# A feature product and a low part on GpSimd, two projections in other empty PSUM banks, query rows loaded first, and instruction lists found anew

## The chip, the cores and the metric

The program runs on one core of one Trainium2 chip. Its time is the device time of one execution in microseconds; the time before is the median of three runs, 313.84 us (313.17 to 314.41).

## The reference

Linear attention is followed by a gated spatial layer, for 4 batches (b), 4 heads, 1088 rows (s) and a head width of 32, all in float32:

```python
a = einsum('rd,bhsd->bhsr', S1, x)                  # 8 features
b = einsum('rd,bhsd->bhsr', S2, x)                  # 8 features
phi(x) = a[..., :, None] * b[..., None, :]          # 64 feature products
q_p, k_p = phi(q), phi(k)
kv = einsum('bhsf,bhsd->bhfd', k_p, v);  z = sum of k_p over s
x  = (q_p . kv) / (q_p . z + 1e-6)                  # joined over heads: (b, s, 128)
h  = relu(x @ w_in);  u, v = h[..., :512], h[..., 512:]
v_n = layer norm of v over its 512 columns
v_s = einsum('ts,bsd->btd', w_spatial, v_n) + b_spatial
out = (u * v_s) @ w_out
```

## The kernel before

**Order.** Every operation is written once with `op(engine, cost, function, reads, writes)` (class `Order`). The text `SEQ` lists all 1922 operations as `name:number@engine`. From it each of five engines (PE, ACT, DVE, POOL and SP, which issues nearly all DMAs) takes its own list and works through it strictly in order, so an operation that waits holds up all that stands behind it in its list. The engine in `SEQ` may be any of an operation's `alts`. `RANK` says in which order the tiles of one tag take the buffers of that tag. A planner's costs decide only where idle PE is given filler matmuls (`FILL`, line 638).

**Stages.** Batch 0 opens the kernel (`attention0`): key rows `kt00` to `kt02` (three groups of 384 rows), values `v00` to `v02` and query rows `qt00` to `qt02` are loaded; `phi` projects a group with the 64 columns of `sk` into a PSUM bank (`kab00`, `qab00`, line 781, 6 matmuls of full float32, which the trace shows as 12 records); ACT copies the a half to SBUF (`ka00`, line 786); DVE multiplies it with the b half, which it reads from PSUM (`kp00`, `qp00`, line 788, 768 products a partition). PE sums keys and values (`kv0:1` to `kv0:3`, line 818), DVE masks the sum (`kd0`, line 842), PE turns the query features (`tq00`, line 863), ACT copies them (`qpT00`, line 867), PE multiplies (`nd00`, line 877), DVE divides (lines 881 to 884), PE turns the result (`xt0`, line 891), and ACT and DVE split it into a high part `xh` and a low part `xl`. Before all that PE runs warm-up matmuls on zeros (`wps`, lines 629 and 633).

**Then** the layer: `pv` (lines 606 to 608, three matmuls for a product of high and low parts), its norm on DVE and ACT, `pu`, the large spatial sums `sp` (lines 1172 to 1183) and the output `po`. The first batch's weights come in meanwhile: `wi_raw1` and `wi_raw0` are halves of `w_in` in float64, turned to float32 in seven steps (`wi_x1:1` to `:7`, lines 673 to 687) and split into `wih` and `wil` (lines 693 and 614 to 617); `wt` are pieces of the spatial matrix, split into `wTh` and `wTl`; the spatial bias comes as two rows (`wTl:10` and `wTl:11`, line 770), copied by DMA out of `bh` and `bl` into the last piece of the matrix, which the last matmuls of a spatial sum read (line 1183). Batches 1 to 3 follow, their attention (lines 927 to 995) laid between the spatial sums of the batch ahead of them.

**Buffers.** PSUM has eight banks: tag `po` 3, `sp` 2, `pu` 1, `sd` 2. All projections of batch 0 use `sd`, so `kab02` and `qab00` wait until a product has read one of its two banks. The tag `g` (three SBUF buffers) holds gated parts of the layer and is empty in the opening.

```python
PS_BUFS = {"po": 3, "sp": 2, "pu": 1, "sd": 2}
ab = bank("sd", f"{what}ab{b}{g}")
```

Of the kernel before, what the change touches and what calls it, by code (L numbers as in the profile page):

```python
# [70 lines left out]
rec1:2@DVE x321:1@DVE pv001:1@PE wTh:4@ACT wi_x0:5@DVE vt00:1@ACT xt1:1@PE wi_x0:6@DVE vt00:2@ACT nd02:1@PE xh0:2@ACT st000:1@DVE wo_raw:1@SP
wi_x0:7@POOL wTh:1@ACT xl0:2@DVE wt60:1@SP pv002:1@PE mv00:1@DVE rec2:1@DVE rec2:2@DVE wTl:1@POOL wih:2@ACT pv010:1@PE x322:1@DVE vt00:3@ACT
st001:1@DVE xt2:1@PE wil:2@POOL vt01:1@ACT pv011:1@PE st002:1@DVE xh0:3@ACT mv00:2@DVE wTh:2@ACT mv00:3@DVE pv012:1@PE xl0:3@DVE wTl:9@POOL vt01:2@ACT
st010:1@DVE pu000:1@PE sd00:1@ACT qt10:1@SP vt01:3@ACT rs00:1@DVE pv020:1@PE t100:1@DVE qt11:1@SP bl:1@DVE u000:1@ACT t100:2@DVE rs00:2@DVE qt12:1@SP
nm00:1@DVE pu010:1@PE vt02:1@ACT vt00:4@DVE wTl:11@SP vt00:5@DVE vh00:1@ACT pv021:1@PE wt70:1@SP vt00:6@DVE u010:1@ACT wt61:1@SP pv022:1@PE vl00:1@DVE
vh00:2@ACT st011:1@DVE pu020:1@PE wo_x:1@ACT vl00:2@POOL wTh:3@ACT sp000:1@PE st012:1@DVE sp010:1@PE vt02:2@ACT mv01:3@DVE sp020:1@PE st020:1@DVE
wTh:7@ACT wTl:12@POOL sp030:1@PE vt02:3@ACT mv01:2@DVE sp010:2@PE st021:1@DVE wTl:2@POOL u020:1@ACT pab10:1@PE mv01:1@DVE st022:1@DVE sd01:1@ACT
pab11:1@PE vh00:3@ACT pu030:1@PE rs01:1@DVE mv02:1@DVE t101:1@DVE abT10:1@ACT mv02:3@DVE t101:2@DVE wTh:11@ACT qd10:1@SP rs01:2@DVE sp020:2@PE
mv02:2@DVE nm01:1@DVE wTh:6@ACT vt01:4@DVE sp000:2@PE wt71:1@SP sd02:1@ACT pab12:1@PE vl00:3@DVE vt01:5@ACT sp030:2@PE rs02:1@DVE wTl:7@DVE vh00:4@ACT
sp030:3@PE t102:1@DVE abT11:1@ACT sp000:3@PE t102:2@DVE vh00:5@ACT vl00:4@DVE sp010:3@PE wTh:5@ACT sp020:3@PE rs02:2@DVE vl00:5@DVE sp030:4@PE  # L80
vt01:6@ACT sp000:4@PE wo_x:2@DVE nm02:1@DVE sp020:4@PE wo_x:3@DVE vh00:6@ACT sp010:4@PE vt02:4@DVE vt02:5@ACT sp010:5@PE vl00:6@DVE sp000:5@PE
vh00:7@ACT wo_x:4@DVE sp030:5@PE sp020:5@PE wTh:13@ACT vl00:7@DVE sp000:6@PE vh00:8@ACT sp010:6@PE wTl:13@DVE wTh:8@ACT sp030:6@PE vl00:8@DVE
vt02:6@ACT wt81:1@SP sp030:7@PE wo_x:5@DVE qd11:2@SP sp000:7@PE wTl:6@DVE vh00:9@ACT sp020:6@PE qd11:1@SP sp010:7@PE wTh:17@ACT vh00:10@DVE sp020:7@PE
wTh:14@ACT sp000:8@PE wo_x:6@DVE wTh:12@ACT sp010:8@PE v91:2@ACT wTl:4@DVE sp020:8@PE kt10:1@SP wTh:18@ACT sp020:9@PE wTl:3@DVE sp000:9@PE v90:2@ACT
sp010:9@PE v93:2@ACT sp010:10@PE wTh:16@ACT sp000:10@PE wTl:14@DVE sp030:8@PE v92:2@ACT wTl:5@DVE abT12:1@ACT sp020:10@PE wt02:1@SP sp030:9@PE
sp000:11@PE wTl:15@DVE sp020:11@PE sp030:10@PE wo_x:7@DVE sp020:12@PE wt12:1@SP sp000:12@PE sp030:11@PE wTl:8@DVE kt11:1@SP sp020:13@PE woh:1@ACT
sp030:12@PE sp000:13@PE kt12:1@SP wTl:18@POOL wTh:15@ACT sp020:14@PE sp030:13@PE sp000:14@PE sp020:15@PE sp000:15@PE wTl:16@POOL wt22:1@SP sp000:16@PE
wTh:19@ACT sp010:11@PE sp010:12@PE sp000:17@PE wTl:21@POOL sp000:18@PE wt32:1@SP sp030:14@PE wTh:20@ACT sp030:15@PE u000:2@DVE sp010:13@PE sp030:16@PE
wTl:20@POOL wTl:19@DVE wt42:1@SP sp030:17@PE g000:1@ACT sp010:14@PE sp020:16@PE qd10:2@SP sp010:15@PE sp020:17@PE sp020:18@PE wt52:1@SP sp030:18@PE
wol:1@POOL sp010:16@PE u020:2@DVE sp010:17@PE wt62:1@SP sp010:18@PE wTl:17@DVE sp001:1@PE qd12:1@SP sp011:1@PE qd12:2@SP sp001:2@PE g000:2@DVE  # L90
sp011:2@PE wt72:1@SP u010:2@DVE wTl:22@POOL u030:1@ACT sp001:3@PE v10:1@SP wTh:21@ACT u030:2@DVE sp001:4@PE g010:1@ACT wt82:1@SP kab10:1@PE v11:1@SP
g010:2@DVE wTh:25@ACT wTh:24@ACT po00:1@PE wTl:27@DVE wTh:23@ACT fa100:1@SP pu001:1@PE wTl:25@DVE po00:2@PE wTl:26@DVE u001:1@ACT fb100:2@SP
g020:1@ACT sp001:5@PE fb100:1@SP ka10:1@ACT sp011:3@PE g020:2@DVE ka11:1@ACT wTh:22@ACT sp001:6@PE fa101:1@SP g030:1@ACT sp011:4@PE v12:1@SP
g030:2@DVE po00:3@PE kp10:1@DVE pu011:1@PE po00:4@PE wTl:24@DVE sp001:7@PE ob00:1@ACT sp001:8@PE fa100:2@POOL wTh:26@ACT out:1@SP sp001:9@PE
wTh:27@ACT sp011:5@PE fb101:1@SP u001:2@DVE fh100:1@ACT sp011:6@PE wTl:28@DVE fb101:2@SP u011:1@ACT sp021:1@PE kp11:1@DVE fl100:1@POOL ka12:1@ACT
gh001:1@ACT fa110:1@SP sp021:2@PE sp011:7@PE fb110:2@SP wTl:23@POOL sp011:8@PE fb110:1@SP sp021:3@PE kp12:1@DVE sp021:4@PE fa111:1@SP sp021:5@PE
fa101:2@POOL fb111:2@SP sp011:9@PE sp021:6@PE u011:2@DVE kt20:1@SP sp021:7@PE fb111:1@SP pu021:1@PE kv1:1@PE u021:1@ACT fh101:1@ACT fl101:1@POOL
sp031:1@PE kd1:4@DVE v20:1@SP fa110:2@POOL kd1:1@DVE kd1:2@DVE sp031:2@PE kd1:3@DVE fa120:1@SP kvh1:1@ACT sp031:3@PE gh011:1@ACT kvl1:1@DVE sp031:4@PE
gl001:1@DVE sp021:8@PE nd100:1@PE nd101:1@PE fh110:1@ACT po01:1@PE x3210:2@ACT fl110:1@POOL sp031:5@PE x3210:1@ACT gl011:1@DVE sp031:6@PE xn10:2@ACT
qt20:1@SP sp021:9@PE xn10:1@ACT fb120:1@SP sp031:7@PE nd101:2@DVE fa111:2@POOL po01:2@PE fa121:1@SP few10:1@DVE u021:2@DVE pu031:1@PE kt21:1@SP  # L100
x3210:3@DVE sp031:8@PE u031:1@ACT fb121:1@SP wTl:29@DVE sp031:9@PE gh021:1@ACT x3210:4@DVE sp002:1@PE fb120:2@SP u031:2@DVE sp002:2@PE xh1:1@ACT
sp002:3@PE xl1:1@DVE sp012:1@PE gl021:1@DVE pu002:1@PE pv100:1@PE pv101:1@PE fa120:2@POOL vt10:1@ACT gh031:1@ACT po01:3@PE st100:1@DVE fh111:1@ACT
pv102:1@PE vt10:2@ACT mv10:1@DVE fl111:1@POOL sp012:2@PE u002:1@ACT st101:1@DVE vt10:3@ACT sp012:3@PE nd110:1@PE mv10:2@DVE gl031:1@DVE nd111:1@PE
fh120:1@ACT po01:4@PE x3211:1@ACT pu012:1@PE x3211:2@ACT xn11:2@ACT qt21:1@SP sp002:4@PE ob01:1@ACT v21:1@SP nd111:2@DVE sp002:5@PE xn11:1@ACT
fb121:2@SP sp002:6@PE few11:1@DVE st102:1@DVE sp012:4@PE out:2@SP x3211:3@DVE sp012:5@PE kt22:1@SP mv10:3@DVE sp002:7@PE x3211:4@DVE sd10:1@ACT
u012:1@ACT sp012:6@PE rs10:1@DVE xh1:2@ACT t110:1@DVE sp002:8@PE xl1:2@DVE sp012:7@PE sp002:9@PE sp012:8@PE u002:2@DVE pv110:1@PE t110:2@DVE
# [1531 lines left out]
```

## Time and profile before

| what | value |
|---|---|
| median of 3 runs | 313.84 us (313.17 to 314.41) |
| the profiled execution, its own time | 313.46 us |
| its span, first to last instruction | 311.7 us |
| time outside the span | 313.46 - 311.7 = 1.76 us |
| granted TensorE clock | 1.000 over the span |
| instructions | 6906 |

A row of the profile names the line of the kernel, the engine, the operation and the tiles (`out<-in`). PE is the matmul array and PEld its weight load; each matmul has one of each. Rows of the timeline begin with the start and the time taken, both in us from the span's start. Matmul records overlap, and their ends are modelled. "issue" stands where an engine waited for nothing that the profile shows.

### The profile page before, as it was taken

The numbers are of one execution on the slowest core, as the hardware profiler recorded it, in microseconds if no ns is written. First come the engines' busy times: TensorE is split into PE (matmuls) and PEld (weight loads), VectorE is DVE, ScalarE is ACT, GpSimd is POOL, SyncE is SP. The second block draws the span as 40 slices with busy tenths as digits, with TensorE's granted clock in tenths as the row PEclk, the third lists the DMA queues.
The fourth block names the chain that finished last, engine by engine and source line by source line (L and its number), as shares of the span: only waits on it lengthen the run. The fifth ranks groups of instructions, "written<-read, shape, count | busy, mean of one in ns | idle before, by whom it ended". The sixth has DMA issues, their size and how long they took to land.

```text
span 311.7 us, 6906 instructions
## 1 busy us (share of the span) xinstructions
PE 305.7 (98%) x2588; PEld 294.7 (95%) x2588; DVE 221.0 (71%) x549; ACT 180.0 (58%) x428; POOL 94.3 (30%) x124
## 2 busy tenths in 40 slices
...
GB/s 243 311 219 161 28 139 207 180 210 103 86 1 23 3 155 158 214 52 0 124 90 141 294 214 117 87 64 84 25 0 2 35 299 0 144 47 0 2 0 72
DMA packets 22989, 33.78 MB, mean 108 GB/s; under 512 B 2988, under 2 KB 21420, under 8 KB 22956
## 3 DMA queue, kind: packets, MB, share of 16 engines
...
q14 instruction: 13, 0.11, 0.1%
HBM read 26.79 MB, written 6.54 MB: 107 GB/s over the span
## 4 chain that ended last, share of the span: by engine, by line
PE 96%; DVE 2%; issue 1%; ACT 0%; DVEq 0%; ACTq 0%
PE sp L1172 15%; PE sp L1174 13%; PE sp L1181 13%; PE sd L1417 9%; PE sp L1417 7%; PE sd L606 4%; PE sd L607 4%; PE sd L608 4%; PE pu L606 3%; PE po L606 3%; PE pu L608 3%; PE pu L607 3%; PE po L607 2%; PE po L608 2%; PE sp L1183 2%; PE sd L781 2%
## 5 line engine op out<-in xcount | busy, mean ns | idle before, releaser
L1172 PE MATMUL sp<-wTh,vh 128*128 128x332 f32 (+1 forms) x286 | 93.7, 329 | 0.0
L1174 PE MATMUL sp<-wTh,vl 128*128 128x332 f32 (+1 forms) x240 | 78.7, 328 | 0.0
L1172 PEld LDWEIGHTS sp<-wTh,vh 128*128 128x128 f32 x286 | 53.7, 188 | 0.5
L1174 PEld LDWEIGHTS sp<-wTh,vl 128*128 128x128 f32 x240 | 45.1, 188 | 0.2
L1181 PE MATMUL sp<-wl,vh 128*128 128x332 f32 x128 | 39.7, 310 | 0.0
L1181 PE MATMUL sp<-wTl,vh 128*128 128x424 f32 x112 | 38.0, 348 | 0.0
L614 DVE TENSOR_TENSOR g<-u,g 128x332 fp32r<-128x332 f32 (+1 forms) x41 | 24.6, 600 | 11.9 <-ACT g L693 6.2
L1165 ACT ACTIVATE u<-pu 128x332 f32<-128x332 f32 (+1 forms) x44 | 20.6, 467 | 19.5 <-PE pu L608 11.7
L1209 DVE TENSOR_TENSOR u<-sp,u 128x332 f32<-128x332 f32 (+1 forms) x43 | 22.3, 521 | 11.7 <-PE sp L1183 10.8
L1013 DVE BATCH_NORM_STATS2 st<-vt 128x6 f32<-128x512 f32 x36 | 24.3, 685 | 8.3 <-ACT vt L1011 8.1
L617 POOL TENSOR_TENSOR r<-pl,r 128x384 fp32r<-128x384 f32 (+1 forms) x18 | 17.8, 996 | 32.0 <-ACT r L693 13.7
L1011 ACT ACTIVATE vt<-sd 128x512 f32<-128x512 f32 x36 | 21.1, 601 | 11.0 <-PE sd L608 10.6
L693 ACT CAST g<-u 128x332 fp32r<-128x332 f32 (+1 forms) x41 | 20.0, 489 | 8.6 <-DVE u L1209 3.5
L950 POOL TENSOR_TENSOR pl<-pl,pl 128x384 f32<-128x384 f32 (+1 forms) x18 | 17.9, 1001 | 21.7 <-DMA pl<-qd 7.6
L1181 PEld LDWEIGHTS sp<-wl,vh 128*128 128x128 f32 x128 | 24.0, 188 | 0.0
L1085 ACT CAST vh<-vt 128x384 fp32r<-128x384 f32 x44 | 21.5, 509 | 1.8 <-DVE vt L1049 1.1
L1181 PEld LDWEIGHTS sp<-wTl,vh 128*128 128x128 f32 x112 | 21.0, 188 | 0.1
L1087 POOL TENSOR_TENSOR vl<-vt,vh 128x384 fp32r<-128x384 f32 (+1 forms) x16 | 14.6, 914 | 21.1 <-ACT vh L1085 16.9
L1052 ACT ACTIVATE vt<-vt,sm,sm 128x512 f32<-128x512 f32 x18 | 14.4, 814 | 3.5 <-DVE sm L1040 3.5
L986 DVE STREAM_TRANSPOSE sd<-c 128x384 f32<-128x384 f32 (+1 forms) x9 | 5.1, 568 | 15.9 <-ACT c L983 15.8
L606 PE MATMUL pu<-xh,wih 128*128 128x332 f32 (+1 forms) x48 | 16.0, 334 | 0.0
L1087 DVE TENSOR_TENSOR vl<-vt,vh 128x384 fp32r<-128x384 f32 (+1 forms) x28 | 14.3, 515 | 2.1 <-ACT vh L1085 2.0
...
## 6 DMA issues: line engine op xcount, KB each, us to landing
...
```

The source lines that it names most:

```text
L606: nc.tensor.matmul(o, ah, bh, start=start, stop=False)
L607: nc.tensor.matmul(o, ah, bl, start=False, stop=False)
L608: nc.tensor.matmul(o, al, bh, start=False, stop=stop)
L614: return lambda: nc.vector.tensor_tensor(out=o(), in0=a(), in1=bb(), op=ALU.subtract)
L1013: op("DVE", 690, lambda stats=stats, t=t: nc.vector.bn_stats(out=stats.ap, in_=vt[:, t]), r=[(vt, t)], w=[stats])
L1085: op("ACT", c_act(384), lambda: nc.scalar.copy(out=vh[:, kk:kk + 3], in_=x()), r=vr, w=[(vh, g)])
L1087: return lambda: eng.tensor_tensor(out=vl[:, kk:kk + n], in0=x()[:, :n], in1=vh[:, kk:kk + n].bitcast(F32), op=ALU.subtract)
L1172: nc.tensor.matmul(sp[:, :cw], vh[:, kt], wTh[:, kt, cs], start=(kt == begin), stop=False)
L1174: nc.tensor.matmul(sp[:, :cw], vl[:, kt], wTh[:, kt, cs], start=False, stop=False)
L1181: nc.tensor.matmul(sp[:, :cw], vh[:, kt], w_lo(kt, c), start=False, stop=False)
L1209: op("DVE", c_dve(cw), lambda: nc.vector.tensor_tensor(out=u.ap, in0=sp[:, :cw], in1=u.ap, op=ALU.mult), r=[sp], w=[u])
L1417: nc.tensor.matmul(x[:, :cw], p, q, start=i == 0 and n == 0, stop=end and i == 3 and n == 2)
```

## The change

- `N_WARM` goes from 6 to 8: two more warm-up matmuls of 128 columns (`wps:8`, `wps:9`).
- In batch 0, `features` has ACT copy both halves of a projection to SBUF (192 elements a partition in place of 96), into a buffer of the tag `g` in place of `ka`. The product may then run on GpSimd (POOL), which reads both halves from SBUF. `SEQ` puts one of the six there, `kp01`. DVE still reads the b half from PSUM.
- `phi` puts the projections `kab02` and `qab00` into a bank of the tag `po`; the other four stay in `sd`.
- `SEQ` and `RANK` are new throughout. Two operations are added (the warm-ups), 110 of the rest change engine: 43 from POOL to DVE, 41 from DVE to POOL, 13 from ACT to DVE, 8 from DVE to ACT, 5 between ACT and POOL. Among them, in the opening, `wi_x1:1` goes from DVE to ACT and the low part `wil:1` from DVE to POOL. DVE has 556 operations after (549 before), ACT 424 (428), POOL 117 (120), PE 644 (642), SP 183 (183).
- PE changes between full float32 and the faster float32 form at 22 places in either list, and the last ten operations of its list are the same.

The heads of the lists, taken from `SEQ`:

```
SP before:   s_raw wi_raw1 kt00 kt01 kt02 v00 mask_sb qt00 v01 b32 v02 ident_sb qt01 qt02 wi_raw0
SP after:    qt00 s_raw wi_raw1 kt00 kt01 kt02 v00 qt01 v01 ident_sb v02 qt02 mask_sb wi_raw0
PE before:   wps.. kab00 kab01 kab02 kv0:1 qab00 kv0:2 kv0:3 tq00 tq01 qab01 qab02 nd00 tq10 tq11 tq20 xt0 tq21 nd01 pv000
PE after:    wps.. kab00 kab01 kab02 qab00 kv0:1 qab01 kv0:2 tq00 tq01 kv0:3 qab02 nd00 tq10 tq11 tq20 xt0 tq21 nd01 pv000
DVE before:  sk:7 wi_x1:1 :2 :3 kp00 eps:2 kp01 kp02 qp00 wi_x1:4 kd0 wi_x1:5 :6 qp01 qp02 rec0 rec0 x320 wi_x0:2 wil:1
DVE after:   sk:7 wi_x1:2 :3 :4 eps:2 kp00 kp02 qp00 wi_x1:5 :6 kd0 qp01 qp02 rec0 rec0 x320 wi_x0:2 :3 xl0
ACT before:  ka00 ka01 ka02 qa00 qpT00 qpT01 qa01 qa02 wi_x0:1 qpT10 wih:1 bh qpT11 xh0
ACT after:   wi_x1:1 ka00 ka01 ka02 qa00 qa01 qpT00 qpT01 qa02 wih:1 qpT10 wi_x0:1 qpT11 xh0
POOL before: v92 v90 v91 wz v93 wi_x1:7 wi_x0:7 wTl:1
POOL after:  v91 v92 kp01 v90 wi_x1:7 wz wil:1 wi_x0:7
SP, bias:    before ... wt21 wTl:10 wt40 ...   after ... wt81 qd11:1 wTl:10 wt02 ...
```

```diff
-N_SMALL, N_WARM = 33, 6
+N_SMALL, N_WARM = 33, 8
...
 SEQ = """
-s_raw:1@SP z9:1@DVE z9:2@DVE wi_raw1:1@SP eps:1@ACT v92:1@POOL wps:1@PE v90:1@POOL kt00:1@SP v91:1@POOL wz:1@POOL kt01:1@SP wps:2@PE kt02:1@SP
-wps:3@PE v93:1@POOL v00:1@SP wps:4@PE sk:1@DVE mask_sb:1@SP wps:5@PE sk:2@DVE sk:3@DVE qt00:1@SP wps:6@PE sk:4@DVE sk:5@DVE wps:7@PE v01:1@SP sk:6@DVE
-sk:7@DVE b32:1@SP wi_x1:1@DVE v02:1@SP wi_x1:2@DVE kab00:1@PE ident_sb:1@SP wi_x1:3@DVE qt01:1@SP kab01:1@PE ka00:1@ACT qt02:1@SP kp00:1@DVE
-ka01:1@ACT eps:2@DVE kp01:1@DVE kab02:1@PE kv0:1@PE ka02:1@ACT wi_raw0:1@SP qab00:1@PE kp02:1@DVE wt30:1@SP qa00:1@ACT wt10:1@SP qp00:1@DVE kv0:2@PE
-wt80:1@SP kv0:3@PE wi_x1:4@DVE tq00:1@PE tq01:1@PE kd0:1@DVE qpT00:1@ACT wi_x1:5@DVE qab01:1@PE qpT01:1@ACT wi_x1:6@DVE qab02:1@PE qa01:1@ACT
-nd00:1@PE qp01:1@DVE wi_x1:7@POOL qa02:1@ACT wi_x0:1@ACT wt01:1@SP qp02:1@DVE wt11:1@SP tq10:1@PE wt50:1@SP tq11:1@PE rec0:1@DVE qpT10:1@ACT wt00:1@SP
...
+qt00:1@SP z9:1@DVE z9:2@DVE s_raw:1@SP eps:1@ACT v91:1@POOL wps:1@PE v92:1@POOL wi_raw1:1@SP kt00:1@SP wps:2@PE kt01:1@SP wps:3@PE kt02:1@SP wps:4@PE
+v00:1@SP wps:5@PE sk:1@DVE qt01:1@SP wps:6@PE sk:2@DVE sk:3@DVE wps:7@PE v01:1@SP sk:4@DVE wps:8@PE sk:5@DVE ident_sb:1@SP sk:6@DVE wps:9@PE sk:7@DVE
+v02:1@SP wi_x1:1@ACT qt02:1@SP kab00:1@PE wi_x1:2@DVE mask_sb:1@SP wi_x1:3@DVE kab01:1@PE ka00:1@ACT wi_x1:4@DVE kab02:1@PE ka01:1@ACT qab00:1@PE
+eps:2@DVE kp00:1@DVE kp01:1@POOL ka02:1@ACT wi_raw0:1@SP wt30:1@SP kp02:1@DVE kv0:1@PE qa00:1@ACT wt80:1@SP qp00:1@DVE qab01:1@PE wt00:1@SP v90:1@POOL
+kv0:2@PE qa01:1@ACT wi_x1:5@DVE tq00:1@PE wi_x1:6@DVE tq01:1@PE qpT00:1@ACT kv0:3@PE qpT01:1@ACT wi_x1:7@POOL qab02:1@PE kd0:1@DVE qp01:1@DVE
+nd00:1@PE qa02:1@ACT wz:1@POOL wt01:1@SP wih:1@ACT qp02:1@DVE wt60:1@SP tq10:1@PE wil:1@POOL wt11:1@SP rec0:1@DVE tq11:1@PE rec0:2@DVE qpT10:1@ACT
...
 RANK = {
...
+    "u212": 49, "u221": 50, "u222": 51, "u231": 52, "u232": 53, "u230": 54, "ob21": 56, "ob22": 55, "ka00": 0, "ka01": 1, "ka02": 2, "qa00": 3,
+    "qa01": 4, "qa02": 5, "gh001": 6, "gl001": 8, "gh011": 7, "gl011": 9, "gh021": 10, "gl021": 11, "gh031": 12, "gl031": 13, "gh002": 14, "gl002":
...
@@ -782,19 +782,27 @@
     def features(b, g, ab, what, at=0, key=None):
-        a_sb = tl("ka", f"{what}a{b}{g}", [P, 3, 32])
-        op("ACT", c_act(96, True), lambda: nc.scalar.copy(out=a_sb.ap, in_=ab_view(ab, at)[:, 0]), r=[(ab, key)], w=[a_sb])
+        both = not b
+        a_sb = tl("g" if both else "ka", f"{what}a{b}{g}", [P, 1 + both, 3, 32])
+        op("ACT", c_act(96 + 96 * both, True), lambda: nc.scalar.copy(out=a_sb.ap, in_=ab_view(ab, at)[:, :1 + both]), r=[(ab, key)], w=[a_sb])
         f = tl("kp", f"{what}p{b}{g}", [P, 3, H * R * R])
-        op("DVE", c_dve(768), lambda: nc.vector.tensor_tensor(
-            out=f.ap.rearrange("p t (h i j) -> p (t h) i j", h=H, i=R),
-            in0=a_sb.ap.rearrange("p t (h i) -> p (t h) i", h=H).unsqueeze(3).broadcast_to([P, 12, R, R]),
-            in1=ab_view(ab, at)[:, 1].rearrange("p t (h j) -> p (t h) j", h=H).unsqueeze(2).broadcast_to([P, 12, R, R]),
-            op=ALU.mult,
-        ), r=[a_sb, (ab, key)], w=[f])
+
+        def product(v, second):
+            return lambda: v.tensor_tensor(
+                out=f.ap.rearrange("p t (h i j) -> p (t h) i j", h=H, i=R),
+                in0=a_sb[:, 0].rearrange("p t (h i) -> p (t h) i", h=H).unsqueeze(3).broadcast_to([P, 12, R, R]),
+                in1=second().rearrange("p t (h j) -> p (t h) j", h=H).unsqueeze(2).broadcast_to([P, 12, R, R]),
+                op=ALU.mult,
+            )
+
+        op(
+            "DVE", c_dve(768), product(nc.vector, lambda: ab_view(ab, at)[:, 1]), r=[a_sb, (ab, key)], w=[f],
+            alts=[("POOL", c_pool(768), product(nc.gpsimd, lambda: a_sb[:, 1]))] if both else [],
+        )
         return f
     def phi(b, g, xt, what):
-        ab = bank("sd", f"{what}ab{b}{g}")
+        ab = bank("po" if (g, what) in ((2, "k"), (0, "q")) else "sd", f"{what}ab{b}{g}")
         op("PE", 650 if (b, g, what) == (0, 0, "k") else 455, f4=True, fn=lambda: project(ab, xt), r=[xt, (sk, "x")], w=[ab])
         return features(b, g, ab, what)
```

## Rows read from the trace of the kernel before

**Rows 1.** The page: busy time by engine, and the chain that ended last.

```profile
PE 305.7 (98%) x2588; PEld 294.7 (95%) x2588; DVE 221.0 (71%) x549; ACT 180.0 (58%) x428; POOL 94.3 (30%) x124
...
PE 96%; DVE 2%; issue 1%; ACT 0%; DVEq 0%; ACTq 0%
```

**Rows 2.** Busy time in three stretches: length, engines (instructions), clock, DMA share, GB/s.

```profile
0.00:16.00 16.00, 13.17 (x328) 11.69 (x329) 12.17 (x28) 5.70 (x15) 3.49 (x10) 1.00 0.87 280
16.00:33.00 17.00, 17.00 (x101) 14.07 (x100) 16.65 (x51) 16.06 (x38) 7.84 (x7) 1.00 0.54 168
33.00:308.00 275.00, 275.00 (x2160) 268.74 (x2161) 191.28 (x470) 158.19 (x378) 82.96 (x107) 1.00 0.30 94
```

**Rows 3.** Timeline of PE, 1 to 18 us: start, us, instructions.

```profile
1.30 1.17 PE L629 MATMUL sd<-u 128*32 128x32 f32 x66 [1.30 <-DVE u L623]
2.40 2.93 PE L633 MATMUL sd<-u 128*128 128x128 f32 x12
5.43 0.77 PE L781 MATMUL sd<-sk,kt 128*64 128x64 f32 x16
...
10.35 0.88 PE L818 MATMUL pu<-v,kp 128*32 128x33 f32 x52 [0.87 <-issue]
11.16 0.87 PE L863 MATMUL po<-u,kp 128*128 128x128 f32 x6
...
12.81 1.55 PE L877 MATMUL sp<-u,c 128*128 128x66 f32 x12
...
15.66 0.55 PE L891 MATMUL sp<-u,c 128*128 128x128 f32 x3 [0.31 <-DVE c L884]
```

**Rows 4.** Timeline of DVE, 2.5 to 16 us.

```profile
2.58 0.55 DVE L675 TENSOR_SCALAR sk<-pl 128x64 uint32<-128x64 uint32 x1 [1.34 <-DMA pl<-in_sks]
...
4.83 0.43 DVE L673 TENSOR_SCALAR vt<-vt 128x512 uint32<-128x512 uint32 x1 [0.23 <-DMA vt<-in_w_in]
...
10.13 0.68 DVE L679 SCALAR_TENSOR_TENSOR vt<-vt,vt 128x512 uint32<-128x512 uint32 x1
...
12.85 1.82 DVE L788 TENSOR_TENSOR kp<-ka,sd 128x768 f32<-128x768 f32 x2 [0.23 <-ACT ka L786]
...
15.05 0.56 DVE L884 TENSOR_TENSOR c<-sp,sm 128x384 f32<-128x384 f32 x1
```

**Rows 5.** Groups by line and form, DVE and POOL: count, busy us, mean ns.

```profile
L788 DVE TENSOR_TENSOR kp<-ka,sd 128x768 f32<-128x768 f32 x6 | 5.6, 953 | 0.5 <-ACT ka L786 0.2
...
L687 POOL TENSOR_TENSOR vt<-vt 128x512 f32<-128x512 f32 x1 | 1.3, 1279 | 9.5 <-DVE vt L685 9.5
```

**Rows 6.** Timeline of ACT in the opening.

```profile
6.04 0.24 ACT L786 COPY ka<-sd 128x96 f32<-128x96 f32 x1 [3.81 <-PE sd L781]
...
13.37 0.68 ACT L673 ACTIVATE v<-kt 128x512 f32<-128x512 f32 x1 [0.20 <-DMA wl<-in_wT]
14.73 0.48 ACT L867 COPY c<-po 128x384 f32<-128x384 f32 x1 [0.69 <-PE po L863]
```

**Rows 7.** Busy time in stretches up to 8 us; the last number is GB/s moved.

```profile
2.00:4.00 2.00, 2.00 (x39) 1.94 (x30) 1.28 (x5) 0.22 (x2) 1.31 (x3) 1.00 0.88 260
4.00:8.00 4.00, 3.65 (x68) 3.06 (x70) 3.51 (x9) 0.55 (x3) 0.00 (x0) 1.00 1.03 351
```

**Rows 8.** The same up to the stop of PE; and line 818's wait instructions on PE.

```profile
0.00:9.30 9.30, 7.65 (x222) 6.89 (x222) 6.25 (x17) 2.44 (x6) 2.21 (x9) 1.00 0.78 251
...
L818 PEldq EVENT_SEMAPHORE  x7: 51/51/51, 10.5 to 164.4; - x7
```

**Rows 9.** Timeline of SP, the DMA issues.

```profile
0.74 0.40 SPq L611 DMA_DIRECT2D pl<-in_sks  x1
1.21 0.41 SPq L611 DMA_DIRECT2D vt<-in_w_in  x1
...
39.05 2.09 SPq L942 DMA_DIRECT2D qd<-abT  x2
```

**Rows 10.** Line 1183: durations, first and last start.

```profile
L1183 PE MATMUL sp<-wTl,v x46: 309/310/356, 46.9 to 306.5; 128*128 128x332 f32 x32, 128*128 128x424 f32 x14
```

276 lines of the change are left out of this document (138 added, 138 removed), and 48 rows, old and new, of the table RANK.

## The prediction

> **What bounds the kernel now.** I read the page first: PE is busy for 98% of the span and makes up 96% of the chain that ended last [rows 1]. A busy PE may still be held up between matmuls, so I then split the span. From 16 to 33 us PE is busy for 17.00 of 17.00 us, from 33 to 308 us for all 275 us; before 16 us it is busy for 13.17 of 16 [rows 2]. Of those 2.83 us, 1.30 pass before PE's first instruction [rows 3], which leaves 1.53 us. The reader is to see that only the opening has time on PE that is plainly idle, and that a new order of the rest can lose time more easily than win it. Between 16 and 33 us DVE (16.65 of 17) and ACT (16.06 of 17) are nearly as full as PE [rows 2].
>
> Third, the timeline of PE in the opening [rows 3]. Warm-ups end at 5.33 us and the first projection starts at 5.43. PE then stops until 10.35 us, for "issue", that is for nothing that the profile shows; of the 52 records that follow, 48 are `kv0:3`, so the stop lies inside `kv0:2`. `tq00` follows at 11.16, `nd00` at 12.81, and `xt0` at 15.66 after a wait for DVE. DVE tells why [rows 4]: four products come before 10.13 us, the last two only at 12.85 to 14.67, and the division ends at 15.61, 0.05 us before `xt0`. So the opening is a chain through DVE's six products of 0.953 us each [rows 5], with one stop of PE in it.
>
> The stop: 222 matmuls and 222 weight loads had run by 9.30 us [rows 8], and the first wait instruction of line 818 starts only at 10.5 [rows 8], after PE has gone on. I read it as PE waiting for its own next instructions, which come by the same DMA engines that moved 351 GB/s then [rows 7]; that 10.5 is also where `kv0:3` had its values `v02`.
>
> **The change part by part.** The sum runs along the chain to `xt0`; what stands behind it is PE's own work and moves with it.
>
> *Query rows first.* `qt00` is 128 x 384 x 4 bytes = 197 kB ahead of all else. At 351 GB/s that is 0.56 us, at the slower 260 GB/s of the start 0.76 [rows 7]; the issue itself takes one slot of 1.21 - 0.74 = 0.47 us [rows 9]. I take 0.5 us for everything behind it: `wi_raw1`, first read at 4.83 [rows 4], at 5.35, `kt00` in time for 5.93 in place of 5.43. The feature matrix `sk` is late by as much, hidden by the warm-ups.
>
> *Two more warm-ups.* Six take 2.93 us [rows 3], so two take under 0.98 us and end between 6.0 and 6.3. With the loads this puts `kab00` at 6.0: 0.57 us later than before. Where the loads come sooner, the warm-ups still hold it.
>
> *`wi_x1:1` to ACT, `:4` ahead of the products.* ACT needs 0.68 us for the like [rows 6]: 5.35 to 6.03. DVE then does two steps of 0.43 and one of 0.68 [rows 4]: to 7.6. Only then comes `kp00`, whose input is ready at 6.0 + 0.61 + 0.32 = 6.93 (0.61 from the start of `kab00` to that of `ka00` [rows 3, 6], 0.32 for the copy, below), so DVE costs 0.67 us here; the step is gone from 10.13 in return.
>
> *Banks and the wider copy.* `kab02` and `qab00` no longer wait for a product, so PE does both by 8.2 (`kt02` is there two loads of 0.56 us after `kt00`). The copy of 192 elements lies between 0.24 us for 96 and 0.48 for 384 [rows 6]: 0.32, 0.08 more, hidden by `wi_x1:4`.
>
> *`kp01` to GpSimd.* DVE has `kp00`, `kp02`, `qp00`: 7.6 + 3 x 0.953 = 10.46 against 10.13 before, with three products done and one beside them. No row shows a product with repeated operands on GpSimd. Below, it is not faster than DVE's 0.953; the nearest row, 512 elements in 1.279 us [rows 5], gives 1.92 in proportion; if repeated reads doubled that, 3.84. I take 1.92, since the operands are two and float32 as in that row: from 7.3, when `ka01` is copied, to 9.2, ahead of its reader. The Trainium skill's page "GPSIMD Engine Reference", section "Performance versus the Vector engine", speaks against such a move: elementwise work with two inputs takes about twice DVE's time there, 4497 ns for 2048 elements, an estimate of 1.69 us for 768 by that page. The sum would be the same by it, because GpSimd has nothing else then: it waits 9.5 us for its step of `wi_x1` [rows 5].
>
> *`kv0:2`, `tq00`.* `qab01` and 24 more instructions of PE now precede `kv0:2`, and 8 of warm-ups, so the same 444 instructions are up at about its 28th of 48 matmuls, at 10.0 us, and PE stops again. If the fetch ends as before, it goes on at 10.35 and ends `kv0:2` at 10.6. The values: with 64 KB for `s_raw` and the identity, 512 for `wi_raw1`, 192 for a group of keys or queries and 198 of values, 1943 KB were queued up to and with `v02`, which was there at 10.5 [rows 8]; 1932 are now queued with `v01`, 1996 with the identity that `tq00` reads (53 more, 0.15 us: 10.65). If `v01` meets what `v02` met, `kv0:2` runs from 10.5 to 11.1. So `tq00` starts at 10.7 or 11.1, against 11.16; I take 10.8.
>
> *On to `xt0`.* `tq00` and `tq01` take 0.7 us, `kv0:3` (its values 251 KB later, 0.73 us, at 11.2) 0.6 to 12.1, `kd0` 0.3 to 12.4. `qp01` and `qp02` follow back to back, since `qab01` was done long before: 12.4 + 1.91 = 14.3 in place of 14.67. From there to `xt0` it took 15.66 - 14.67 = 0.99 us, hence 15.3: 0.36 us gained. With `v01` late it is 15.75, 0.1 lost; with nothing late at all `v02` still holds `kv0:3`, and the gain is 0.45. I take **0.3 us**.
>
> *`wil:1` to GpSimd.* 1.28 us there as in [rows 5], after `wi_x1:7` and `wz`: done by 15.3, and its reader `pv000` starts after 17. It takes 0.68 us off DVE when that is full.
>
> *The new lists.* Behind 33 us 275 us of 275 are busy: nothing to gain, and each wait made there adds its length. 110 operations change engine, but DVE is busy for 191 of those 275 us, ACT 158 and GpSimd 83 [rows 2]; most such moves hide behind PE. I take 0; above, one missed hand-over costs what PE's stop in the opening costs, 10.35 - 9.3 = 1.05 us.
>
> The sum: 0.3 us less. The profiled execution, 311.7 of span and 1.76 around it, 313.46, would take 313.16; the median of the runs, 313.84, lies 0.38 above it, hence **313.5 us**.
>
> **The rivals.**
>
> *Nothing is kept* (313.8, up to 314.4). `v01` comes late as above, or GpSimd needs 3.84 us for `kp01`: from 7.3 to 11.1, `kv0:2` behind it to 11.7, and `xt0` at 16.2, 0.5 late. Or PE is earlier by 0.3 at 16 us and DVE and ACT, full until 33, hand it back. For it: the nearness of 1932 and 1943 KB. Against: DVE has lost about 2.06 us of work there (a product, `wi_x1:1`, `wil:1`: 0.95 + 0.43 + 0.68).
>
> *The bias row comes late* (slower). `wTl:10` was issued early; now it stands behind `qd11:1` in SP's list, which before was over at 39.05 + 2.09 = 41.14 us [rows 9]. A DMA on an empty queue needs 1.84 us from issue to use (0.74 to 2.58, the first load and the first step of `sk` [rows 4, 9]). So it lands near 43, and line 1183, which reads it, starts at 46.9 [rows 10]. Up to 3.9 us of delay on SP cost nothing; beyond that PE and all behind it stand, one us for one. For 315.5 or more SP must be 5.9 us late. For it: SP is held by buffers there, and GpSimd and DVE, which free them, have new lists. Against: the margin.
>
> *More is won* (312.3 or less). If all of the 1.53 us went, 313.84 - 1.53 = 312.3. Against: the same loads must come through a queue at its full rate, and the chain through DVE and the stop remain.
>
> **How the numbers follow.** Front earlier by 0.1 to 0.5, rest as before: 0.62. Nothing kept: 0.21. Bias row or another new wait: 0.11, of which 0.09 over 0.5%. More won: 0.06, most of it over 0.5% (0.05). A measurement of this kernel can tell about 0.5%, 1.57 us, from no change. So faster 0.05, same 0.86, slower 0.09. The range reaches down to the whole 1.53 us, 312.3, and up to one missed hand-over of 1.05 us with nothing kept, 314.9, the bound of the lists.
>
> **What would show it.** `kab00` near 6.0 us; products on DVE from 7.6; `kp01` on GpSimd in 1.92 us, over before 9.3; a stop of PE inside `kv0:2` until 10.35; `tq00` at 10.8, `nd00` at 12.6, `xt0` at 15.3; PE without a listed wait behind 16 us. The prediction is wrong if `xt0` starts after 15.66, if the stretch behind 33 us is longer than 275 us by more than 0.5, or if PE's clock falls below 1.00 in the opening.

## The result, and the profile after

The changed kernel takes **315.53 us** (median of 6 runs, 314.76 to 315.57) where the kernel before takes 313.36 beside it (6 runs, 312.84 to 314.41): a ratio of 1.0061, 95% interval 1.0042 to 1.0080. It is slower by 2.2 us. I had forecast 313.5, at most 314.9.

The profiled execution took 315.57 us with a span of 313.8, against 311.7. First, what PE waited for in the changed kernel (line, releaser, us in all, times, longest); the 1.3 us at the top are its start.

```profile
PE sd L629 <- DVE u L623: 1.3, 1, 1.3
PE sd L781 <- DMA kt<-in_kT: 1.1, 1, 1.1
PE po L607 <- DVE g L614: 0.8, 1, 0.8
PE pu L826 <- DVE kp L791: 0.7, 1, 0.7
PE pu L826 <- issue: 0.7, 1, 0.7
```

Three of these are new: 1.1 us for keys, 0.7 us for the first product `kp00`, and 0.8 us for `g` in the output product of line 607. The busy times by stretch, columns as in [rows 2], show that PE is no longer full behind 16 us:

```profile
0.00:16.00 16.00, 12.14 (x322) 11.11 (x323) 9.35 (x23) 5.50 (x13) 5.71 (x11) 1.00 0.86 272
16.00:33.00 17.00, 16.87 (x102) 14.07 (x100) 15.67 (x49) 16.39 (x38) 8.48 (x8) 1.00 0.52 161
33.00:308.00 275.00, 274.10 (x2155) 266.78 (x2154) 197.51 (x481) 155.54 (x373) 79.58 (x103) 1.00 0.30 95
```

**Where the time went.** The last row hides how the lag grows, so I counted, in both traces, the matmul columns behind the warm-ups and fillers (658,464 in each) and took the time at which the same number had begun. The table gives how much later that is than in the kernel before, at seven of its times; the other kernels are those of the experiments.

```
kernel, in us later, at     16.8   96.3  184.3  196.0  254.5  272.4  302.0
changed                     1.02   0.75   0.82   1.24   1.27   2.00   2.10
e2, query rows first alone  1.50   1.21   1.23   1.24   1.23   0.99   0.85
e4, new lists from 40 us    0.05   0.36   0.62   1.03   1.07   2.05   2.13
e10, new lists from 162 us -0.52   0.47   0.36   0.77   1.02   1.60   1.41
e5, old lists from 162 us   1.36   1.09   1.53   1.53   1.55   1.54   1.32
e6, sums earlier            0.51   0.70   0.83   1.25   1.28   1.39   1.20
e9, e5 with query later    -0.31  -0.58  -0.10  -0.10   0.04   0.12  -0.11
```

So the changed kernel loses 1.02 us in the opening, 0.42 between 184 and 196 us, and 0.73 between 254 and 272; 0.2 come back in between. Each row is one execution: e10, which has the lists of the kernel before up to 162 us, is 0.52 us ahead of it at 17 us and 0.47 behind at 96. A step of a few tenths is read here only where several kernels with the same lists show it.

**The opening**, engine by engine, in the order of time, against [rows 3, 4, 6]:

```profile
6.39 0.67 ACT L673 ACTIVATE vt<-vt 128x512 f32<-128x512 f32 x1 [4.16 <-DMA vt<-in_w_in]
...
7.04 0.97 PE L781 MATMUL sd<-sk,kt 128*64 128x64 f32 x24 [1.10 <-DMA kt<-in_kT]
...
8.63 0.95 DVE L791 TENSOR_TENSOR kp<-g,sd 128x768 f32<-128x768 f32 x1
...
8.88 1.51 POOL L791 TENSOR_TENSOR kp<-g 128x768 f32<-128x768 f32 x1 [7.03 <-DVE eps L650]
...
9.49 1.83 DVE L791 TENSOR_TENSOR kp<-g,po 128x768 f32<-128x768 f32 x2
...
9.63 0.63 PE L826 MATMUL pu<-v,kp 128*32 128x33 f32 x48 [0.73 <-DVE kp L791]
...
11.87 0.34 PE L826 MATMUL pu<-v,kp 128*32 128x33 f32 x17 [0.72 <-issue]
...
12.13 0.87 PE L871 MATMUL po<-u,kp 128*128 128x128 f32 x6
...
14.05 1.52 PE L885 MATMUL sp<-u,c 128*128 128x66 f32 x12
...
15.15 1.27 POOL L617 TENSOR_TENSOR wil<-vt,wih 128x512 fp32r<-128x512 f32 x1 [0.23 <-DMA wl<-in_wT]
...
16.69 0.55 PE L899 MATMUL sp<-u,c 128*128 128x128 f32 x3
```

The reader is to see that the chain keeps its shape and starts late. `wi_raw1` is there for its first step at 6.39 us in place of 4.83, the keys for `kab00` at 7.04 in place of 5.43, and PE, which is through with its warm-ups at 5.95, waits 1.10 us for them. The first product waits for the steps of `wi_x1` and starts at 8.63; PE stops again inside `kv0:2`, until 11.87 in place of 10.35; `xt0` is at 16.69 in place of 15.66. From 2 to 4 us the DMA engines moved 232 GB/s and from 4 to 8 us 311, against 260 and 351 in [rows 7]:

```profile
2.00:4.00 2.00, 2.00 (x40) 1.94 (x30) 0.56 (x3) 0.22 (x2) 0.00 (x0) 1.00 0.83 232
4.00:8.00 4.00, 2.90 (x37) 2.63 (x35) 1.75 (x7) 0.98 (x2) 0.00 (x0) 1.00 0.98 311
```

**At 266 us.** Three blocks of values (`vt62`, `vt61`, `vt60`, 768 KB each) are loaded back into buffers whose last readers are the sums `s121:3` to `s121:6`. SP's line covers its three issues; the others are `s121:6`, the first readers of the last block, the sum `e12:3`, `gl312`, and the matmul that reads it:

```profile
249.74 4.82 SPq L1492 DMA_DIRECT2D vt<-vd  x3
...
253.93 0.28 DVE L1255 TENSOR_TENSOR kvh<-vt,kvh 128x128 f32<-128x128 f32 x1
...
260.22 0.51 ACT L1093 CAST vh<-vt 128x384 fp32r<-128x384 f32 x1 [2.71 <-DMA vt<-vd]
...
260.29 0.42 DVE L1255 TENSOR_TENSOR kvh<-vt,vt 128x256 f32<-128x256 f32 x1 [1.47 <-DMA vt<-vd]
...
266.11 0.50 DVE L1441 TENSOR_TENSOR pl<-sd,pl 128x332 f32<-128x332 f32 x1
...
266.53 0.63 DVE L614 TENSOR_TENSOR g<-u,g 128x332 fp32r<-128x332 f32 x1
...
267.21 0.42 PE L607 MATMUL po<-g,woh 128*128 128x332 f32 x1 [0.80 <-DVE g L614]
```

And in the kernel before, where DVE reads the last block at 256.42 without a wait and `gl312`, started at 264.55, is done at 265.04, 0.26 us ahead of the matmul of line 607 that reads it:

```profile
248.00 3.15 SPq L1484 DMA_DIRECT2D vt<-vd  x3
...
264.55 0.49 DVE L614 TENSOR_TENSOR g<-u,g 128x332 fp32r<-128x332 f32 x1
...
265.30 0.31 PE L607 MATMUL po<-g,woh 128*128 128x332 f32 x1
```

SP's last issue is over at 254.56 instead of 251.15, because `s121:6`, which now stands behind `u311:2`, `x60:2`, `x60:3` and `gl302` too on DVE, ends only at 254.21. ACT then waits 2.71 us and DVE 1.47 for that block. From there DVE is nearly full, busy for 6.27 of 6.81 us, and `gl312` starts 6.24 us behind DVE's first reader (266.53 - 260.29), too late for PE.

### The profile page after: what moved, and what is told of

Same layout as the page of the kernel before. It is cut to its first block, busy times and chain, and to the rows that moved or that the text cites. A ratio compares the mean times of both kernels' runs of the same rounds, so it can differ in the third digit from the quotient of the medians.

```text
span 313.8 us, 6908 instructions
## 1 busy us (share of the span) xinstructions
PE 305.7 (97%) x2588; PEld 294.2 (94%) x2588; DVE 224.3 (71%) x556; ACT 177.9 (57%) x424; POOL 93.8 (30%) x121
## 4 chain that ended last, share of the span: by engine, by line
PE 88%; DMA 5%; DVE 3%; SPq 2%; ACT 1%; issue 1%; DVEq 0%
PE sp L1180 15%; PE sp L1189 12%; PE sp L1182 12%; PE sd L1425 7%; PE sp L1425 5%; PE sd L606 4%; PE sd L608 4%; PE sd L607 4%; PE pu L606 3%; PE po L607 2%; PE pu L607 2%; PE pu L608 2%; PE po L606 2%; PE po L608 2%; PE sp L1191 2%; DMA vt<-vd 2%
## 5 line engine op out<-in xcount | busy, mean ns | idle before, releaser
L614 DVE TENSOR_TENSOR g<-u,g 128x332 fp32r<-128x332 f32 (+1 forms) x41 | 23.2, 566 | 7.5 <-PE po L607 3.0
L1095 DVE TENSOR_TENSOR vl<-vt,vh 128x384 fp32r<-128x384 f32 (+1 forms) x35 | 19.6, 568 | 2.2 <-ACT vh L1093 2.1
L607 PE MATMUL pu<-xl,wih 128*128 128x332 f32 (+1 forms) x48 | 15.6, 326 | 0.0
L608 PE MATMUL pu<-xh,wil 128*128 128x332 f32 (+1 forms) x48 | 15.6, 326 | 0.0
L1191 PE MATMUL sp<-wTl,v 128*128 128x332 f32 (+1 forms) x46 | 14.8, 323 | 0.0
```

The lines of the kernel that those rows point to most:

```text
L607: nc.tensor.matmul(o, ah, bl, start=False, stop=False)
L608: nc.tensor.matmul(o, al, bh, start=False, stop=stop)
L614: return lambda: nc.vector.tensor_tensor(out=o(), in0=a(), in1=bb(), op=ALU.subtract)
```

## The experiments

The two kernels share most of `SEQ`, so lists can be cut and joined. The column "step" is the start of the first step of `wi_x1`, "reload" the start of the first instruction that waits for the last block of values, "g" what PE waits for `g` at 266 us; medians of the kernel before, run beside, are in brackets. The ratios are not those of the medians (e10: 1.0015 and 1.0033). A new list also changes the planner's fillers: e1, e9 and e12 have two filler matmuls (four records) more than the changed kernel, between 8.9 and 9.9 us.

```
run                              us median [before]   ratio (95%)              step  xt0    reload  g
e1  query rows later             315.99 [313.54]  1.0070 (1.0043 to 1.0096)  5.56  16.29  261.15  0.7
e2  before, query rows first     314.50 [313.54]  1.0036 (1.0015 to 1.0058)  6.37  17.17  257.96  none
e3  old lists from 40 us         316.11 [313.54]  1.0081 (1.0060 to 1.0103)  6.92  16.47  259.25  none
e4  new lists from 40 us         316.29 [313.54]  1.0088 (1.0053 to 1.0122)  5.35  15.72  260.26  0.9
e5  old lists from 162 us        314.73 [313.79]  1.0025 (1.0006 to 1.0044)  6.39  17.03  258.59  none
e10 new lists from 162 us        314.82 [313.79]  1.0015 (0.9994 to 1.0036)  5.01  15.14  259.72  0.6
e6  sums earlier                 314.70 [313.79]  1.0022 (1.0002 to 1.0042)  6.63  16.17  259.58  none
e8  keys first                   314.80 [313.79]  1.0028 (1.0012 to 1.0044)  9.70  16.42  259.19  none
e9  e5 with query rows later     313.77 [313.55]  1.0003 (0.9989 to 1.0016)  4.80  15.35  257.55  none
e7  e5 with kp01 on DVE          314.94 [313.55]  1.0045 (1.0029 to 1.0061)  6.24  16.64  259.08  none
e12 sums earlier, query later    314.04 [313.55]  1.0013 (0.9995 to 1.0031)  5.06  16.36  258.44  none
e11 keys and values first        316.85 [313.55]  1.0101 (1.0073 to 1.0129)  9.66  16.98  260.48  none
```

**e1 and e2: the query rows.** One move undone in the changed kernel, the same move alone in the kernel before:

```diff
-qt00:1@SP s_raw:1@SP wi_raw1:1@SP kt00:1@SP kt01:1@SP kt02:1@SP v00:1@SP qt01:1@SP
+s_raw:1@SP wi_raw1:1@SP kt00:1@SP kt01:1@SP kt02:1@SP v00:1@SP qt00:1@SP qt01:1@SP
```

```diff
-s_raw:1@SP wi_raw1:1@SP kt00:1@SP kt01:1@SP kt02:1@SP v00:1@SP mask_sb:1@SP qt00:1@SP
+qt00:1@SP s_raw:1@SP wi_raw1:1@SP kt00:1@SP kt01:1@SP kt02:1@SP v00:1@SP mask_sb:1@SP
```

> The changed kernel with one move undone: qt00 stands behind v00 in SP's list and no longer ahead of all loads. Theory (query rows first cost more than the 0.5 us that I gave them): wi_raw1 lands near 4.8 us and kt00 near 5.3 as before, kab00 starts by 6.0 behind the warm-ups, xt0 near 15.3 to 15.7, and the time falls by 1.0 to 1.4 us, to 314.1 to 314.5, since the wait at 266 us stays. Rival (the load comes late whatever stands first, and the longer chain through ACT, DVE and GpSimd is what costs): wi_raw1 may land earlier, but xt0 stays after 16.3 and the time above 315.0.

> The kernel before with qt00 alone put ahead of all other loads. Theory: wi_raw1 lands 1.3 to 1.6 us later than in the kernel before (near 6.2), the first step of wi_x1 and the first product with it, xt0 moves from 15.66 to 16.5 or more, and the time grows by 0.8 to 1.4 us, to 314.2 to 314.8. By the term of my prediction the loads are 0.5 us late, xt0 near 16.1 and the time 313.8. Rival (the load is late in the changed kernel for another reason): xt0 within 0.2 us of 15.66.

e2 is as the theory said: the move alone puts `xt0` 1.5 us later and costs 1.0 us (1.0036). The timeline of its opening:

```profile
6.37 0.43 DVE L673 TENSOR_SCALAR vt<-vt 128x512 uint32<-128x512 uint32 x1 [1.27 <-DMA vt<-in_w_in]
...
7.03 0.96 PE L781 MATMUL sd<-sk,kt 128*64 128x64 f32 x24 [1.03 <-DMA kt<-in_kT]
...
11.98 0.76 PE L818 MATMUL pu<-v,kp 128*32 128x33 f32 x56 [0.93 <-issue]
...
17.17 0.55 PE L891 MATMUL sp<-u,c 128*128 128x128 f32 x3 [0.31 <-DVE c L884]
```

e1 is a miss, on the time and on the opening. The loads came earlier (5.56, not 4.8) and `xt0` by 0.40 us, at 16.29 and not by 15.7, next to the rival's 16.3. Its last block of values was there only at 261.15, 0.93 later than in the changed kernel, though SP issued it at the same time, and PE waited 0.7 us for `g` and 0.6 for a sum of line 1425. A gain in the opening can be lost again at that wait; hence e9 and e12 below.

**e3, e4, e5, e10: the lists.** Up to an operation each engine has the list of one kernel, behind it that of the other; at `sp000:8` (some 40 us) and at `sp122:9` (162 us). The part of DVE's list on which the loads of values depend, old to new:

```diff
-e10:3@DVE wil:8@DVE x40:6@DVE s121:5@DVE s121:6@DVE u311:2@DVE gl301:1@DVE x60:2@DVE
+e10:3@DVE x40:6@DVE s121:4@DVE u311:2@DVE x60:2@DVE wil:8@DVE s121:5@DVE x60:3@DVE gl302:1@DVE s121:6@DVE
```

> The changed kernel up to its operation sp000:8 (some 40 us), and from there each engine's list in the order, and on the engines, of the kernel before. Theory (two separate losses): the opening keeps its loss, xt0 at 16.7, the wait of 0.8 us for g at 266 us is gone, and the time is 314.3 to 314.8. Rival (the wait at 266 us follows from the opening being late, not from the lists): the wait is there again and the time is 315.2 to 315.8.

> The kernel before up to its operation sp000:8 (some 40 us), and from there the lists of the changed kernel. Theory: xt0 at 15.66 as before, a wait for g of 0.7 to 1.0 us near 265 us, and 0.9 to 1.4 us more than the kernel before: 314.3 to 314.8. Rival (the lists cost nothing by themselves): 313.1 to 313.7.

> The changed kernel up to its operation sp122:9 (near 162 us), and from there the lists of the kernel before; at this point the two kernels have started nearly the same operations, so the seam of the first attempt at 40 us is gone. Theory (the late loss of 1.2 to 1.4 us comes from the new lists behind 162 us): no wait for g at 266 us, PE no later against the kernel before at 300 us than it was at 160 us, and 314.1 to 314.6. Rival (the loss is that of the late opening, or of lists ahead of 162 us): 315.2 or more.

> The kernel before up to sp122:9, and from there the lists of the changed kernel. Theory: the opening is that of the kernel before, PE loses 0.4 us near 189 us and about 1 us near 266 us, and the time is 314.6 to 315.2. Rival (the lists behind 162 us cost nothing without the late opening): 313.2 to 313.8.

e4 says that the lists cost by themselves: opening as before (0.05 us), the waits at 189 and 266 us there, 315.70 in the profiled execution and 316.29 in the median, more than I expected. Some of that is its seam, where the two lists meet: PE falls back by 0.46 us between 30 and 36 us, where four filler records run (33.37 to 33.70). e3 is inconclusive: the wait at 266 us is gone, but where its two halves meet, at 47 us, PE falls back by another 1.2 us; six filler records run there. At 162 us the seam is cleaner, and there the traces of both directions agree. e5 has no wait for `g`, and behind its seam, which takes 0.3 us (1.21 at 161 us, 1.54 at 167), PE loses nothing more; it takes 314.73, 0.13 over what was expected. The old lists are not free of this loss, though. In e7, e8 and e11 below, which have them too, the last block was read 0.5 to 1.9 us later than in e5, and PE waited 0.2, 0.3 and 1.0 us between 261 and 264 us for `u` of line 1217, which DVE works out behind that block; by the count above it lost 0.40, 0.57 and 1.29 us between 254.5 and 272.4 us. SP's last issue ended there no more than 0.5 us later than in e5, so most of the delay is the load's own. The rows of e5's loads:

```profile
249.55 3.15 SPq L1492 DMA_DIRECT2D vt<-vd  x3
...
258.59 0.42 DVE L1255 TENSOR_TENSOR kvh<-vt,vt 128x256 f32<-128x256 f32 x1 [0.54 <-DMA vt<-vd]
```

e10 loses 0.41 us by 196 and 0.6 at 266, yet stands at 1.0015, with an interval that takes in 1: its runs go from 313.31 to 315.45, five of twelve below 314, which I read as a wait at 266 us that comes in some executions only; with one of them profiled, that is not shown. It shows too that a gain in the opening is handed back: PE was 0.52 us ahead at 17 us and then waited for DVE:

```profile
15.14 0.55 PE L891 MATMUL sp<-u,c 128*128 128x128 f32 x3 [0.31 <-DVE c L884]
...
22.14 0.56 DVE L884 TENSOR_TENSOR c<-sp,sm 128x384 f32<-128x384 f32 x1
...
22.76 0.55 PE L891 MATMUL sp<-u,c 128*128 128x128 f32 x3 [0.49 <-DVE c L884]
```

**e6: the reload.** Three operations moved on DVE's list of the changed kernel, nothing else:

```diff
-s121:4@DVE u311:2@DVE x60:2@DVE wil:8@DVE s121:5@DVE x60:3@DVE gl302:1@DVE s121:6@DVE
+s121:4@DVE u311:2@DVE wil:8@DVE s121:5@DVE s121:6@DVE x60:2@DVE x60:3@DVE gl302:1@DVE
```

> The changed kernel with three operations moved on DVE's list: wil:8, s121:5 and s121:6 stand ahead of x60:2, so that the last readers of the rows of values that are replaced end about 1.2 us earlier. Theory (the wait at 266 us is the third reload of values, issued only when s121:6 is done, and what then queues on ACT and DVE): the last of the three loads is issued near 253 us in place of 254.2, the wait for g falls by 0.4 us or more, and the time by 0.4 to 1.0 us, to 314.5 to 315.1. Rival (gl312 is late because e12:3 and the low parts stand ahead of it, whenever the load lands): the wait and the time stay, 315.3 to 315.8.

```profile
249.75 3.59 SPq L1492 DMA_DIRECT2D vt<-vd  x3
...
259.58 0.52 ACT L1093 CAST vh<-vt 128x384 fp32r<-128x384 f32 x1 [2.06 <-DMA vt<-vd]
...
259.65 0.43 DVE L1255 TENSOR_TENSOR kvh<-vt,vt 128x256 f32<-128x256 f32 x1 [0.82 <-DMA vt<-vd]
...
265.88 0.64 DVE L614 TENSOR_TENSOR g<-u,g 128x332 fp32r<-128x332 f32 x1
```

The issues are over at 253.34, the block is read 0.64 us earlier, `gl312` starts 6.23 us behind that as in the changed kernel, and the wait is gone: 314.70, ratio 1.0022 in place of 1.0061, 1.2 us by the ratios. `e12:3` still stands ahead of `gl312`, so the rival falls. Whether `gl312` ahead of `e12:3`, as in the old lists, would have done it too was not run. The margin is thin: with new lists the reload was read at 259.72 (e10, 0.6 us of wait) and at 259.58 (e6, none).

**e9 and e12: both losses taken away.** e9 is e5 with the edit of e1; e12 is e6 with `qt00` behind `kt02`.

> The kernel of old lists from 162 us (314.73 us, against 313.79 for the kernel before) with qt00 behind v00 in SP's list. Theory (what is left of the loss is the query rows ahead of all loads): wi_raw1 lands near 5.2 us in place of 6.4, xt0 comes 0.4 to 0.8 us earlier, the time falls by 0.3 to 0.8 us, to 313.9 to 314.4. Rival (the opening's other parts cost it): 314.6 to 315.0.

> The changed kernel with both repairs: wil:8, s121:5 and s121:6 ahead of x60:2 (314.70 us by itself), and qt00 behind kt02 in SP's list, ahead of v00. Theory (the two losses add): kab00 near 6.0 us, no wait for g at 266 us, 313.9 to 314.4. Rival (the opening's gain is given back): 314.6 or more.

By the ratios e9 is 0.7 us faster than e5, and e12 0.3 us faster than e6, though the intervals overlap in both pairs. e12 still spreads, from 313.44 to 315.53, six of twelve runs below 314, so something comes and goes there that its one trace does not show. e9, a little below its forecast, equals the kernel before (1.0003), with all of the change's work on GpSimd and in the other banks of the opening left in, and with a seam that takes 0.3 us. Its opening, without a listed stop of PE:

```profile
4.80 0.67 ACT L673 ACTIVATE vt<-vt 128x512 f32<-128x512 f32 x1 [2.57 <-DMA vt<-in_w_in]
...
8.03 0.57 PE L781 MATMUL po<-sk,c 128*64 128x64 f32 x12 [0.42 <-DMA c<-in_qT]
...
10.23 0.63 PE L826 MATMUL pu<-v,kp 128*32 128x33 f32 x48
...
15.35 0.55 PE L899 MATMUL sp<-u,c 128*128 128x128 f32 x3
```

**e7: the product on GpSimd.**

```diff
-kp01:1@POOL kp00:1@DVE kp02:1@DVE
+kp00:1@DVE kp01:1@DVE kp02:1@DVE
```

> The kernel of old lists from 162 us (314.73 us) with the product kp01 back on DVE, between kp00 and kp02. By my prediction (GpSimd's time for it lies beside DVE's): qp00 ends 0.95 us later, tq00 comes later by 0 to 0.5 us, since PE's stop covers part of it, and the time is 314.7 to 315.3. Rival (the product on GpSimd holds PE): the time falls by 0.3 us or more, to 314.4 or less.

1.0045 against 1.0025, with intervals that overlap: putting it back gains nothing, so no sign is left that the product on GpSimd held PE. What it wins is not told apart from zero: the profiled execution of e7 has `xt0` 0.39 us earlier than that of e5, and lost 0.40 us at the last block of values.

**e8 and e11: a better opening?** On e5: keys and queries ahead of `wi_raw1`, the steps of `wi_x1` behind the products (on ACT behind its copies), and five warm-ups; e8's lists:

```diff
-qt00:1@SP s_raw:1@SP wi_raw1:1@SP kt00:1@SP kt01:1@SP kt02:1@SP v00:1@SP qt01:1@SP
+s_raw:1@SP kt00:1@SP kt01:1@SP kt02:1@SP qt00:1@SP v00:1@SP wi_raw1:1@SP qt01:1@SP
...
-wi_x1:2@DVE wi_x1:3@DVE wi_x1:4@DVE eps:2@DVE kp00:1@DVE kp02:1@DVE qp00:1@DVE wi_x1:5@DVE
+eps:2@DVE kp00:1@DVE kp02:1@DVE qp00:1@DVE wi_x1:2@DVE wi_x1:3@DVE wi_x1:4@DVE wi_x1:5@DVE
```

> The kernel of old lists from 162 us with another opening: the keys, qt00 and v00 are loaded ahead of wi_raw1, ACT makes its copies ahead of wi_x1:1, DVE its three products ahead of wi_x1:2 to 4, and there are five warm-ups in place of eight. Theory (what bounds the opening is when the keys land, then PE's stop, which follows it): kab00 near 5.0 us, the stop over by 9.6, tq00 near 9.9, xt0 between 14.3 and 15.0, and 312.0 to 313.0. Rival (the steps of wi_x1, or the values and the rows behind them in the queue, then hold the chain): xt0 at 15.7 or later and 313.3 or more.

> The kernel of old lists from 162 us with keys, qt00, v00 and qt01 ahead of wi_raw1, five warm-ups, both kp01 and qp01 on GpSimd, and on DVE the steps wi_x1:2 to 4 behind qp00, then kd0. In the kernel with keys first (314.80 us) kab00 started at 4.84 us, but qt01 landed at 10.21 and v01 at 11.18, behind wi_raw1 (9.68), and PE waited 1.0 and 0.4 us for them. Theory (the loads in the order in which the chain reads them are the bound): qt01 lands near 7.5, v01 near 9.7, tq00 starts by 10.5, xt0 at 14.3 to 15.2 and the time is 312.3 to 313.4. Rival (PE's stop after 448 instructions, or the bias steps on DVE, holds the chain at the old place): xt0 at 15.7 or later, 313.6 or more.

e8 has `kab00` at 4.84 us as expected and then waits for what now stands behind `wi_raw1`:

```profile
4.84 1.32 PE L781 MATMUL sd<-sk,kt 128*64 128x64 f32 x24
...
10.34 0.57 PE L781 MATMUL sd<-sk,c 128*64 128x64 f32 x12 [1.02 <-DMA c<-in_qT]
...
11.31 0.62 PE L826 MATMUL pu<-v,kp 128*32 128x33 f32 x48 [0.40 <-DMA v<-in_vA]
```

In both the time is the rival's. e11 loads those earlier and has no listed stop of PE, but the planner puts 24 records of filler matmuls into PE's list where it expects idle time, the last ten right ahead of `nd00` (line 638), and `xt0` comes at 16.98. The opening is less than half of e11's loss: PE is 1.32 us late at 16.8 us and 3.29 at 272, of which 1.29 us come at the late block of values, shown in the last row. Neither beats the kernel before, nor does any other kernel here.

```profile
8.93 1.83 PE L638 MATMUL po<-u 128*128 128x128 f32 x14
...
13.19 1.38 PE L638 MATMUL po<-u 128*128 128x128 f32 x10
...
14.41 1.45 PE L885 MATMUL sp<-u,c 128*128 128x66 f32 x12
...
263.18 0.42 PE L1425 MATMUL sp<-xl,vh 128*128 128x332 f32 x1 [1.03 <-DVE u L1217]
```

## Why the prediction was wrong

**"Query rows first ... I take 0.5 us"** is the step that failed in the opening: it measured 1.56 us at the first step of `wi_x1` (6.39 against 4.83) and 1.61 at `kab00` (7.04 against 5.43). I divided the bytes of `qt00` by a rate, 0.56 us at 351 GB/s. Yet more than that is lost: in the DMA records the first packet of the large load starts at 2.74 us in place of 2.27, about the 0.5 us that I took, but from 3.0 to 3.5 us the queue finished 29 KB in place of 144. By 5 us 727 KB had come in against 849, although the queue began at the same time. The Trainium skill (DMA: Bandwidth & Descriptors, "Queues, rings and completion order") says that each DMA engine takes its descriptors in the order of the ring; the traces agree, as the loads right behind `qt00` are all late: the first reader of `s_raw` by 0.79 us (3.37 against 2.58), the other two by 1.56 and 1.61. Nor is the single profile a fixed point: over the kernels here the first step starts at 6.24 to 6.92 us with query rows first (six kernels, median 6.39) and at 4.80 to 5.56 without (six, median 5.04). The medians lie 1.35 us apart; my term was well under half of that, and the profile that I read was one of the two earliest. Why the rate falls in the first microseconds stays open.

**"If the fetch ends as before, it goes on at 10.35"** failed with it. PE stops behind the same 449th recorded instruction in eight of the fourteen traces, but not at the same time. In the trace's DMA records a packet of 16 KB of instructions comes first, for an engine that they do not name; PE goes on 1.26 to 1.46 us after it has ended, and where that is early enough, there is no stop. Seven of the fourteen:

```
kernel      kab00   packet ends   PE stops      goes on
before      5.43        8.92        9.28         10.35
e4          5.96        9.08       10.02         10.45
e9          5.74        8.87        none
e12         5.70       10.10       10.36         11.48
e1          6.16        9.95       10.75         11.41
changed     7.04       10.53       10.95         11.87
e2          7.03       10.67       10.85         11.98
```

In the changed kernel and in e2, whose loads are late, the packet is late too, and the stop with it: 1.52 us later than forecast. Loads are not all of it, since e12 has early keys and a late packet; what sets its start stays open. Products on DVE began at 8.63 in place of 7.6, `kp01` was over at 10.39 and not by 9.3, `tq00` came at 12.13 for 10.8, `xt0` at 16.69 for 15.3. The stop is not the whole of it: e6, with the same lists in the opening and `kab00` at 7.29, has no listed stop, and `xt0` at 16.17.

**"The new lists ... I take 0; above, one missed hand-over"** is the second failure, and its bound, 1.05 us, was about the size of what came: 0.42 between 184 and 196 us and 0.73 between 254 and 272. I argued with DVE's 191 busy us in 275, an average. What counted was one chain in one place: the last reader of a buffer, a load of 768 KB that waits for it, and a full DVE behind that load. The wait at 189 us, where a new order on PE asks for a bank that DVE frees only at 189.27, I saw in each kernel with new lists behind 162 us and in none with old ones; it was not taken apart further. It is seen on the weight load:

```profile
188.77 0.50 DVE L1217 TENSOR_TENSOR u<-sp,u 128x332 f32<-128x332 f32 x1 [0.29 <-ACT u L1173]
...
189.33 0.19 PEld L1180 LDWEIGHTS sp<-wTh,vh 128*128 128x128 f32 x1 [0.45 <-DVE u L1217]
```

**The rest stood.** Warm-ups end at 5.95 (forecast 6.0 to 6.3, near enough); the first step of `wi_x1` takes ACT 0.67 us (0.68); `kab02` and `qab00` wait for no product; `wil:1` is off DVE and hidden, though it ends at 16.42 and not by 15.3. With the keys ahead of the query rows the gain that I forecast came in one of three traces: e9 has `xt0` at 15.35, 0.31 us before [rows 3], where I said 0.36 and took 0.3; e1, whose opening has the same lists, has it at 16.29, and e12 at 16.36, both with a stop of PE. That e9 meets the number is therefore no proof of the sum. The seam of e9 takes as much again, so its time doesn't show the gain either.

**The product on GpSimd** took 1.51 us, between my bounds and below the 1.92 taken; the Trainium skill's GPSIMD Engine Reference ("Performance versus the Vector engine"), from which I had estimated 1.69, is nearer, and still high for operands that repeat.

**The rivals.** "Nothing is kept" fell short: 313.8 to 314.4 has no room for two losses. "The bias row comes late" did not happen: its DMA was issued at 43.14 us, its first reader ran at 48.3 without a wait. The result lies with "another new wait", to which I gave 0.11 together with the bias row. Two of the three signs that I had named against me came true: `xt0` after 15.66, and a stretch behind 33 us longer by 1.16 us (0.94 at 37 us, 2.10 at 302). The third did not: PE's clock is 1.00 in the row of the opening.
